# Q and K of two more row tiles as seven block products, and new places in the engines' lines

## The chip, the cores and the metric

The kernel runs on one core of one Trainium2 chip. Its time is the device time of one execution in microseconds (us), given as the median of several runs. Engines: PE (TensorE, matmuls), DVE (VectorE), ACT (ScalarE), POOL (GpSimd), SP (SyncE, which here only issues the transfers).

## The reference

One layer on x of 2048 rows by 512 columns, in float32: a layer norm, a local dilated attention, a second layer norm, and a GeGLU feed-forward part.

```python
qkv = layernorm(x) @ wqkv                       # 2048 x 1536: q, k, v; 32 heads of 16
idx = pos[:, None] - arange(8)[None, :] * 2     # each row sees 8 rows, 2 apart
attn = softmax(where(idx >= 0, (q . k[idx]) * 16 ** -0.5, -1e9))
h = x + (attn . v[idx]) @ wo
n = layernorm(h)
out = h + (gelu(n @ w_gate) * (n @ w_up)) @ w_down   # 512 -> 1792 -> 512
```

## The kernel before

**Tiles and chunks.** The 2048 rows are four chunks (c = 0 to 3) of 512, each of four row tiles (j = 0 to 3) of 128. The 512 columns are four blocks of 128 (k). The feed-forward part goes over 14 blocks of 128 of its 1792 columns.

**Matmuls in three parts.** Each float32 operand is held as a high part that the matmul unit takes as it is, and a low part, the rest: `split` (L343) makes both, the high one by a cast on ACT, the low one by a subtraction on DVE or POOL (L346). A product is then three matmuls, high by high, high by low and low by high. An output tile of 128 x 512 over 512 columns is 3 x 4 = 12 matmuls of 128x128 weights and 512 columns; the helper `mm` (L409, its matmuls at L424) issues them in three groups of four.

**The projections.** Rows are normalized and transposed to `xT` (high and low, `prep`, L517). V comes from `project` (L699), Q and K from `project_pair(c, p)` (L608), which takes the row tiles j0 = 2p and j1 = 2p + 1 together. For a pair, K and Q (s = 1 and 0) of two tiles are four outputs of 128 x 512. There are two branches. A pair in `PLAIN` takes the direct one: four outputs of twelve matmuls, each copied out by ACT (L625). Every other pair is seen as a 2 x 2 block product (tiles by halves of the columns, halves by Q and K) that is done in seven block products instead of eight, in Winograd's form: `product` (L642) is six matmuls (L649), three accumulators `qka`, `qkb`, `qkc` collect them, ACT copies four sums out (`scaled`, L661), and DVE adds three more onto what was copied (`added`, L666). The seven products need sums of the weights, made once (`weight_sums`, L567: wsa, wsb, then wT_2 to wT_5, split at L586 and L587), and for each pair sums of the rows (`sums`, L544): four additions of 128x256 (L554 to L557), two casts (L560) and two subtractions (L561) into `xS` and `xSl`. The sum wT_5 lies where weights of the direct branch lie (wh_0, wl_0), so as long as a pair is in `PLAIN` it is held back until that pair is through.

**The stages.** K and V go to memory, are read back at eight offsets (kw, vw), and `attention` (L725) works on DVE, POOL and ACT: `pk` = kw * qp (L762), a reduction to logits (L765), a softmax, `pv` = vw * probabilities (L806), halving additions (L811, L813). `tail(c)` (L835) turns the result to oT, multiplies by wo (high and low wo_h, wo_l), adds x, normalizes to `xhat_h` and transposes that (tp_h) to hT (hTh, hTl). In `ffn_step`, pg and pu are the gate and up products, g their combination, and acc the product with w_down. The attention of chunk 0 runs beside the projections of chunks 1 to 3; the later ones beside the feed-forward part of the chunk before. The feed-forward parts of chunks 2 and 3 run together for seven pairs of blocks (`joint`, L1026), again with seven products; `combine` (L995) makes the sums of rows for that (traw, L1011 to L1017, split to tt, tth and ttl at L1020 and L1021), tile after tile as the transposes of chunk 3 come.

**What sets the order.** The code doesn't emit instructions directly: each goes as an operation into `Plan`, with an engine, an estimated duration and what it reads and writes. `schedule` (L204) lists them by rank, the longest path to the end, engine by engine; on the chip each engine works its line in that order. Two tables adjust it: an entry of `SHIFTS` (first operation, how many, engines, nanoseconds) adds to the ranks of a run of operations, and a number in `SWAPS` puts an operation on its other engine (DVE or POOL for those added by `either`, ACT or DVE for those by `evict`). Transfers are all issued by SP.

Of the kernel before, what the change touches and what calls it, by code (L numbers as in the profile page):

```python
# [58 lines left out]
PLAIN = ((1, 0),)  # L59
# [9 lines left out]
    (1243, 51, "DVE POOL", 607), (1684, 47, "PE", 2887), (439, 11, "PE", -722), (1244, 116, "POOL", 519), (1484, 6, "DVE", 150411),  # L69
    (1712, 19, "PE", 3415), (1355, 6, "PE DVE ACT POOL SP", 453), (1818, 14, "DVE POOL", 1438), (420, 49, "DVE", -1515), (1271, 1, "DVE POOL", 1503),  # L70
    (805, 72, "PE DVE ACT POOL SP", 65), (1659, 45, "POOL", 4286), (1329, 5, "DVE POOL", 1248), (474, 21, "PE DVE ACT POOL SP", 83),
    (1945, 18, "PE", -716), (447, 33, "POOL", -774), (1674, 94, "PE DVE ACT POOL SP", 350), (438, 33, "DVE POOL", -523), (610, 3, "DVE", -1930),
    (1714, 11, "DVE POOL", -1835), (1574, 208, "DVE", -1090), (480, 8, "DVE", 431), (1306, 3, "DVE", -9919), (2055, 13, "PE DVE ACT POOL SP", 7868),
    (456, 2, "SP", 1705), (1285, 100, "POOL", -927), (476, 12, "POOL", -381), (452, 26, "PE", 4811), (809, 1, "PE DVE ACT POOL SP", 5603),
    (1354, 295, "SP", 347), (1358, 300, "POOL", 1339), (763, 183, "POOL", -78), (1185, 30, "DVE", 499), (1224, 84, "SP", -702),
    (890, 137, "POOL", 2449), (1739, 3, "ACT", 17332), (832, 16, "DVE", -177), (349, 16, "DVE", 8493), (198, 121, "SP", -12152),
    (1995, 136, "DVE", 10496), (1876, 12, "PE DVE ACT POOL SP", 603), (1865, 220, "DVE", 332), (1597, 2, "PE", 3205), (617, 37, "POOL", 446),
    (796, 2, "PE DVE ACT POOL SP", 4277), (693, 197, "PE", -649), (1304, 285, "DVE", -348), (1358, 129, "ACT", -838), (2054, 35, "DVE POOL", 9076),
    (1343, 13, "DVE", -308), (991, 177, "DVE", -621), (1335, 25, "POOL", 1698), (1202, 44, "PE", 121), (1172, 93, "DVE", -308), (1211, 3, "DVE", 830),
    (1052, 105, "ACT", -3324), (1261, 40, "DVE", -1436), (2058, 18, "PE", 8276), (2059, 1, "PE DVE ACT POOL SP", -15914),  # L80
    (113, 159, "PE DVE ACT POOL SP", 1041), (725, 67, "DVE POOL", -248), (826, 143, "SP", 1028), (573, 15, "PE DVE ACT POOL SP", 1449),
    (628, 3, "PE DVE ACT POOL SP", 1298), (1577, 7, "PE", -3666), (1370, 14, "PE", -1291), (305, 55, "ACT", 785), (832, 2, "PE DVE ACT POOL SP", 694),
    (266, 3, "DVE POOL", -4610), (986, 174, "DVE POOL", 371), (1209, 56, "SP", -365), (1093, 219, "SP", -672), (719, 170, "SP", -647),
    (1116, 2, "PE DVE ACT POOL SP", 506), (1227, 41, "DVE POOL", 71), (187, 75, "PE DVE ACT POOL SP", 2353), (1262, 42, "PE DVE ACT POOL SP", 530),
    (251, 3, "PE", -2556), (363, 3, "DVE POOL", -11034), (1802, 193, "DVE POOL", -111), (667, 6, "PE", -703), (1048, 234, "POOL", -100),
# [164 lines left out]
def tile_block(ctx: ExitStack, tc: tile.TileContext, x: bass.AP, xt: bass.AP, wqkv: bass.AP, wo: bass.AP,  # L250
# [266 lines left out]
    def prep(c, j):  # L517
        mb, mv = means[c]
        xc = raw(f"xc_{c}_{j}")
        if c in CROSS_X:  # L520
# [46 lines left out]
    def weight_sums():  # L567
# [9 lines left out]
        for i, (src, r, slot) in {3: (T1, (ra, 0), "gu0"), 4: (T2, (ra, 1), "more"), 2: (T4, (rb, 0), "wo_h"), 5: (T3, (rb, 1), None)}.items():  # L577
# [10 lines left out]

            if slot or not PLAIN:
                put()  # L590
# [17 lines left out]
    def project_pair(c, p):  # L608
# [5 lines left out]
        mv = means[c][1]  # L614
        if (c, p) in PLAIN:
            for s in (1, 0):
# [697 lines left out]
```

## Time and profile before

| | |
|---|---|
| median of 3 runs | 636.82 us (636.06 to 637.57) |
| the profiled execution, its own time | 637.77 us |
| its span | 636.0 us |
| TensorE clock granted, mean | 0.999 |
| first matmul of a projection, start | 11.62 us |
| last matmul, start | 631.59 us |

The span runs from the first to the last instruction that the profiler recorded; 1.77 us of the execution lie around it. "Busy" of an engine is the time in which it had an instruction at work. Matmuls overlap: a row of one matmul has 0.39 us, while the next starts 0.23 us after it, so PE's pace is read from starts. A row of the timeline is: start, duration, engine, line, operation, output<-inputs, shape, how many; in brackets the idle time of the engine just before it and what ended it. A row of the waits is: engine and line that waited, <- engine and line waited for, microseconds in total, times, the longest. Rows of grouped lines end in: busy time, mean ns of one, idle time before.

### The profile page before, as it was taken

Reading aid. Unit: us, or ns where it says so; the run is one execution under the profiler, and the core shown is the slowest. Engines: PE = TensorE matmul, PEld = TensorE weight load, DVE = VectorE, ACT = ScalarE, POOL = GpSimd, SP = SyncE. Lnnn points to the kernel's source line nnn. Section 1 sums busy time; section 2 is a strip of 40 time slices with the busy share of each in tenths; the row PEclk is TensorE's granted clock in tenths of the full one; section 3 lists DMA queues with packets and bytes.
Section 4 is the critical chain, followed back from the end, with each engine's and each line's share of the span. In section 5 each row is a group of like instructions: output and inputs, shape, how many; then the busy total and the mean of one; then the engine's idle time right before and its main releaser. Section 6 shows DMA issues by size and latency. Waiting matters only on the chain.

```text
span 636.0 us, 8302 instructions
## 1 busy us (share of the span) xinstructions
PE 627.6 (99%) x2794; PEld 514.8 (81%) x2794; DVE 490.2 (77%) x533; ACT 411.7 (65%) x702; POOL 390.0 (61%) x356
## 2 busy tenths in 40 slices
PE   9999999999999999999999999999999999999997
PEld 8888888877888887788888888887788888888885
DVE  5989999989999799989999999958775353343421
ACT  5796597457645954996876787976546555543542
POOL 4758788755799799344595882966737765720000
PEclk9999999999999999999999999999999999999999
DMA  8657697698879858999999689941232332212672
GB/s 307 235 196 267 207 259 216 193 361 279 321 245 290 280 190 230 291 330 371 336 294 330 184 260 251 262 133 36 88 107 103 116 99 84 66 51 54 197 223 89
DMA packets 74330, 134.04 MB, mean 211 GB/s; under 512 B 32288, under 2 KB 32544, under 8 KB 73904
## 3 DMA queue, kind: packets, MB, share of 16 engines
q1 hardware_dynamic: 74288, 133.51, 65.9%
q8 instruction: 22, 0.36, 0.2%
q14 instruction: 20, 0.16, 0.1%
HBM read 99.88 MB, written 26.80 MB: 199 GB/s over the span
## 4 chain that ended last, share of the span: by engine, by line
PE 79%; DVE 7%; DMA 4%; POOL 4%; ACT 4%; issue 1%; ACTq 0%; SPq 0%; DVEq 0%; POOLq 0%
PE pa L1086 10%; PE qkv L424 10%; PE pu L424 7%; PE pg L424 7%; PE acc L900 6%; PE acc L902 6%; PE acc L901 6%; PE pc L1086 5%; PE wo L424 5%; PE qka L649 4%; DMA fraw<-in_wffn_dram 2%; PE qkc L649 2%; PE qkv L417 2%; PE pb L1086 2%; PE warm_ps L332 2%
## 5 line engine op out<-in xcount | busy, mean ns | idle before, releaser
L811 POOL TENSOR_TENSOR pv<-pv 128x1024 f32<-128x1024 f32 (+1 forms) x46 | 92.2, 2012 | 21.3 <-DVE pv L806 20.6
L900 PE MATMUL acc<-dnh,gh 128*128 128x512 f32 x224 | 87.4, 390 | 0.0
L902 PE MATMUL acc<-dnh,gl 128*128 128x512 f32 x224 | 87.2, 389 | 0.0
L901 PE MATMUL acc<-dnl,gh 128*128 128x512 f32 x224 | 87.1, 389 | 0.0
L762 DVE TENSOR_TENSOR pk<-kw,qp 128x2048 f32<-128x2048 f32 x32 | 72.8, 2279 | 3.0 <-DMA kw<-kv 2.0
L806 DVE TENSOR_TENSOR pv<-vw,qp 128x2048 f32<-128x2048 f32 x32 | 72.7, 2281 | 0.9 <-ACT qp L785 0.5
L765 DVE TENSOR_REDUCE lg<-pk 128x128 f32<-128x2048 f32 x32 | 72.6, 2278 | 0.2
L424 PE MATMUL pg<-hTh,gu 128*128 128x512 f32 x224 | 60.2, 390 | 0.0
L424 PE MATMUL pu<-hTh,gu 128*128 128x512 f32 x224 | 59.9, 389 | 0.0
L424 PEld LDWEIGHTS pg<-hTh,gu 128*128 128x128 f32 x224 | 41.8, 188 | 9.6 <-ACT g L951 0.4
L900 PEld LDWEIGHTS acc<-dnh,gh 128*128 128x128 f32 x224 | 42.0, 188 | 9.0 <-ACT acc L304 0.2
L902 PEld LDWEIGHTS acc<-dnh,gl 128*128 128x128 f32 x224 | 42.1, 188 | 8.8
L424 PEld LDWEIGHTS pu<-hTh,gu 128*128 128x128 f32 x224 | 42.0, 188 | 8.8
L901 PEld LDWEIGHTS acc<-dnl,gh 128*128 128x128 f32 x224 | 42.1, 188 | 8.6
L346 POOL TENSOR_TENSOR gl<-g,gh 128x512 fp32r<-128x512 f32 x24 | 32.1, 1340 | 12.9 <-ACT gh L345 12.9
L1072 POOL TENSOR_TENSOR jl<-fraw,jh 128x256 fp32r<-128x256 f32 (+1 forms) x21 | 20.8, 994 | 27.6 <-ACT jh L1071 14.3
L345 ACT CAST gh<-g 128x512 fp32r<-128x512 f32 x42 | 26.0, 619 | 17.7 <-DVE g L957 9.8
L1118 ACT COPY jt<-pa 128x512 f32<-128x512 f32 x36 | 21.1, 587 | 24.8 <-PE pa L1086 20.2
L915 ACT CAST dnh<-fraw 128x512 fp32r<-128x512 f32 x42 | 25.9, 619 | 14.8 <-PE acc L902 8.8
L1086 PE MATMUL pa<-tt,jh 128*128 128x512 f32 x112 | 30.4, 393 | 1.4 <-ACT tt L1020 0.7
L1072 POOL TENSOR_TENSOR jl<-sraw,jh 128x512 fp32r<-128x512 f32 x21 | 27.3, 1302 | 6.6 <-ACT jh L1071 6.6
L346 POOL TENSOR_TENSOR gu<-fraw,gu 128x512 fp32r<-128x512 f32 x20 | 26.2, 1321 | 7.0 <-ACT gu L345 7.0
(312 smaller groups left out, 1600.2 us busy)
## 6 DMA issues: line engine op xcount, KB each, us to landing
fraw<-in_wffn_dram SPq DMA_DIRECT2D x45, 768.0 KB, 5.2
kw<-kv SPq DMA_DIRECT2D x16, 704.0 KB, 6.0
vw<-kv SPq DMA_DIRECT2D x16, 704.0 KB, 5.2
dnl<-ld SPq DMA_DIRECT2D x42, 256.0 KB, 3.0
gu<-ld SPq DMA_DIRECT2D x17, 512.0 KB, 5.4
kv<-qkvt SPq DMA_DIRECT2D x32, 256.0 KB, 4.2
ld<-gu SPq DMA_DIRECT2D x14, 512.0 KB, 4.5
x<-in_x_dram SPq DMA_DIRECT2D x16, 256.0 KB, 5.0
```

Source lines behind the costliest of these rows:

```text
L346: sub = lambda eng: eng.tensor_tensor(lo(), src(), hi().bitcast(F32), op=ALU.subtract)
L424: nc.tensor.matmul(acc(), a, b, start=(p == k == 0 and not seeded), stop=(p == n - 1 and k == KD - 1), skip_group_check=seeded)
L649: nc.tensor.matmul(acc(), a(k), b()[:, k], start=first and q == k == 0, stop=q == 2 and k == 1, skip_group_check=not first)
L762: nc.vector.tensor_tensor(pr(), k4, q2.unsqueeze(2).to_broadcast([P, 2, W, QF]), op=ALU.mult)
L765: dve(2195, lambda pr=pr, jj=jj: nc.vector.tensor_reduce(lg()[:, i, jj:jj + 2], pr().rearrange("p j w (h d) -> p j w h d", d=DH), axis=AX. ...
L806: nc.vector.tensor_tensor(pr().rearrange("p j w (h d) -> p j w h d", d=DH), v5, e5, op=ALU.mult)
L811: either(home, 256 * m, lambda eng, pr=pr, m=m: eng.tensor_tensor(pr()[:, :, 0:m], pr()[:, :, 0:m], pr()[:, :, m:2 * m], op=ALU.add), [], ...
L900: nc.tensor.matmul(a, gh()[:, sl], dh(), start=(i == 0 and not SEED), stop=False, skip_group_check=SEED)
L901: nc.tensor.matmul(a, gh()[:, sl], dl(), start=False, stop=False, skip_group_check=SEED)
L902: nc.tensor.matmul(a, gl()[:, sl], dh(), start=False, stop=(i == NF - 1), skip_group_check=SEED)
L1072: either("POOL", (hi - lo) * 256, lambda eng, src=src, v=v, W_=W_, L_=L_: eng.tensor_tensor(v(L_), src(), v(W_).bitcast(F32), op=ALU.subtr ...
L1086: nc.tensor.matmul(acc(), a[:, k], b(k), start=first and p == k == 0, stop=p == 2 and k == 1, skip_group_check=not first)
```

## The change

Line 59 empties `PLAIN`: the pair (1, 0), the first two row tiles of chunk 1, was the only one in the direct branch, and goes to the seven products like the other seven pairs. With it, `prep` calls `sums` for that pair too, and `weight_sums` splits wT_5 at once. The tables `SHIFTS` and `SWAPS` are renewed as a whole; the first has eight lines fewer, so that all lines behind it have numbers lower by 8.

```diff
-PLAIN = ((1, 0),)
+PLAIN = ()
...
-    (1243, 51, "DVE POOL", 607), (1684, 47, "PE", 2887), (439, 11, "PE", -722), (1244, 116, "POOL", 519), (1484, 6, "DVE", 150411),
...
+    (1249, 51, "DVE POOL", 607), (1250, 116, "POOL", 519), (1490, 6, "DVE", 150411), (1824, 14, "DVE POOL", 1410), (426, 49, "DVE", -670),
...
-    74, 81, 191, 194, 260, 262, 364, 365, 370, 372, 474, 484, 490, 491, 492, 494, 496, 571, 586, 602, 610, 613, 614, 615, 629, 640, 650, 652,
...
+    74, 77, 81, 92, 228, 262, 266, 267, 269, 370, 371, 376, 378, 387, 480, 490, 496, 497, 498, 500, 502, 577, 588, 592, 597, 606, 608, 619, 620,
...
```

PE's line has 2788 matmuls where it had 2794, DVE's 528 rows for 535, POOL's 376 for 361, ACT's 691 for 688; SP issues 328 transfers in both.

In the rows of the lines below, the chunk is left out of a name and a running number stands last.

The first place is PE's line between 45 and 60 us of the profile, where chunk 1 is projected. Before (qkv_1_0 is K of tile 0, qkv_0_1 Q of tile 1; qka_1 belongs to the second pair):

```order
L424 MATMUL qkv_0_1_613<-wh_242,xTh_1_536 128x512 x4
L424 MATMUL qkv_0_0_622<-wh_242,xTh_0_530 128x512 x4
L649 MATMUL qka_1_632<-wh_142,xTh_2_547 128x512 x2
L649 MATMUL qka_1_632<-wl_150,xTh_2_547 128x512 x2
L649 MATMUL qka_1_632<-wh_142,xTl_2_605 128x512 x2
L424 MATMUL qkv_0_0_622<-wl_254,xTh_0_530 128x512 x4
L424 MATMUL qkv_0_1_613<-wl_254,xTh_1_536 128x512 x4
L424 MATMUL qkv_0_0_622<-wh_242,xTl_0_586 128x512 x4
```

Of the change (qkc_0, qka_0 and qkb_0 belong to the first pair):

```order
L641 MATMUL qka_1_608<-wh_142,xTh_2_576 128x512 x2
L641 MATMUL qka_1_608<-wl_150,xTh_2_576 128x512 x2
L641 MATMUL qka_1_608<-wh_142,xTl_2_585 128x512 x2
L641 MATMUL qkc_0_621<-wT_304,xS_0_522 128x512 x4
L641 MATMUL qkc_0_621<-wT_304,xSl_0_539 128x512 x2
L416 MATMUL qkv_2_0_637<-wh_352,xTh_0_533 128x512 x4
L641 MATMUL qka_0_648<-wh_142,xTh_0_533 128x512 x2
L641 MATMUL qka_0_648<-wl_150,xTh_0_533 128x512 x2
L641 MATMUL qka_0_648<-wh_142,xTl_0_632 128x512 x2
```

The two pairs of chunk 1 now run mixed with one another, and twelve groups of four are replaced by seven products of six.

The second place is DVE's line ahead of wo of chunk 0, from 128 us on. Before (tp_o is the transposed attention output of the last tile, wor the wo weights as loaded):

```order
L666 SCALAR_TENSOR_TENSOR qkvt_1_1195<-qkb_1_1313,mvx_500,qkvt_1_1195 128x4x128
L762 TENSOR_TENSOR pk_1_0_1335<-kw_1_1080,qp 128x2048
L346 TENSOR_TENSOR oTl_1119<-tp_o_3_0_1338,oTh_1078 128x256
L666 SCALAR_TENSOR_TENSOR qkvt_0_1253<-qkc_1_1341,mvx_500,qkvt_0_1253 128x4x128
L346 TENSOR_TENSOR wo_l<-wor_998,wo_h 128x512
L346 TENSOR_TENSOR oTl_1119<-tp_o_3_2_1361,oTh_1078 128x256
L666 SCALAR_TENSOR_TENSOR qkvt_0_1253<-qkc_1_1341,mvx_500,qkvt_0_1253 128x4x128
L346 TENSOR_TENSOR wo_l<-wor_1013,wo_h 128x512
```

Of the change:

```order
L338 TENSOR_TENSOR oTl_1189<-tp_o_3_0_1307,oTh_1054 128x256
L805 TENSOR_TENSOR o_3_1295<-pv_3_2_1247 128x256
L658 SCALAR_TENSOR_TENSOR qkvt_1_1180<-qkb_1_1310,mvx_526,qkvt_1_1180 128x4x128
L754 TENSOR_TENSOR pk_1_0_1344<-kw_1_1065,qp 128x2048
L338 TENSOR_TENSOR oTl_1189<-tp_o_3_2_1334,oTh_1054 128x256
L658 SCALAR_TENSOR_TENSOR qkvt_0_1263<-qkc_0_1131,mvx_526,qkvt_0_1263 128x4x128
L658 SCALAR_TENSOR_TENSOR qkvt_0_1263<-qkc_1_1357,mvx_526,qkvt_0_1263 128x4x128
L338 TENSOR_TENSOR wo_l<-wor_991,wo_h 128x512
L338 TENSOR_TENSOR wo_l<-wor_1075,wo_h 128x512
```

The last oTl stands right behind pk, and the first wo_l split has gone behind it and behind two additions. o_3 (from POOL) is new on DVE ahead of pk.

The third place is DVE's line in the joint stage, from 440 us on, up to pa's multiplication by its mask (L1124; L1116 of the change). Before (traw_4187 belongs to tile 1, traw_4238 to tile 2, traw_4284 to tile 3):

```order
L405 TENSOR_SCALAR xhat_h_3_4254<-h_4049,mv_h_3_4227,rs_h_3_4232 128x512
L346 TENSOR_TENSOR hTl_4132<-tp_h_2_4222,hTh_4117 128x4x128
L1021 TENSOR_TENSOR tt_4148<-traw_4187,tt_4148 128x2x128
L1021 TENSOR_TENSOR tt_4152<-traw_4187,tt_4152 128x2x128
L1021 TENSOR_TENSOR ttl_4210<-traw_4187,tth_4197 128x2x128
L1011 TENSOR_TENSOR traw_4284<-tp_h_3_4270,hTh_3580 128x256
L1012 TENSOR_TENSOR traw_4284<-traw_4284,hTl_3605 128x256
```

Of the change (traw_4194, traw_4247 and traw_4295 are tiles 1 to 3):

```order
L338 TENSOR_TENSOR hTl_4135<-tp_h_2_4232,hTh_4124 128x4x128
L1006 TENSOR_TENSOR traw_4247<-tp_h_2_4232,traw_4247 128x256
L1007 TENSOR_TENSOR traw_4247<-tp_h_2_4232,traw_4247 128x256
L397 TENSOR_SCALAR xhat_h_3_4277<-h_4059,mv_h_3_4244,rs_h_3_4254 128x512
L1013 TENSOR_TENSOR tt_4150<-traw_4194,tt_4150 128x2x128
L1003 TENSOR_TENSOR traw_4295<-tp_h_3_4285,hTh_3571 128x256
L1004 TENSOR_TENSOR traw_4295<-traw_4295,hTl_3587 128x256
```

Two splits of tile 1 (tt_4152 and ttl_4210 of before) have gone to POOL. The splits and additions further on (tt and traw of tiles 2 and 3) are divided anew between DVE and POOL, too: two of them leave DVE ahead of L1124, and a 128x512 split (jl) comes in. On PE, the transpose tp_h of tile 3 stands three matmuls later.

More of the change, by code (lines that the diff above doesn't have):

```diff
@@ L73 @@
[L73 to L84, printed above, removed]
```

70 lines of the change are left out of this document (37 added, 33 removed), and 8 rows, old and new, of the table SWAPS.

## The prediction

> **What bounds the kernel now.** I read the page's first and fourth parts, then the windows by stage, the waits of TensorE (PE), and the timelines around the longest of them.
>
> ```profile
> span 636.0 us, 8302 instructions
> PE 627.6 (99%) x2794; PEld 514.8 (81%) x2794; DVE 490.2 (77%) x533; ACT 411.7 (65%) x702; POOL 390.0 (61%) x356
> ...
> PE 79%; DVE 7%; DMA 4%; POOL 4%; ACT 4%; issue 1%; ACTq 0%; SPq 0%; DVEq 0%; POOLq 0%
> ```
>
> PE is busy for 627.6 of 636.0 us, and the chain that ended last runs through PE for 79%. A matmul that disappears therefore shortens the span, unless PE then stands at a place where another engine is no earlier than before. The windows show where such places can be (the pairs are busy time and instructions of PE, PEld, DVE, ACT and POOL, then the clock, the DMA share and GB/s):
>
> ```profile
> 36.00:154.00 118.00, 117.43 (x524) 95.36 (x523) 112.39 (x111) 80.91 (x144) 84.05 (x75) 1.00 0.75 240
> 154.00:425.00 271.00, 270.25 (x1189) 221.91 (x1188) 250.42 (x231) 198.75 (x315) 193.05 (x154) 1.00 0.87 274
> 425.00:452.00 27.00, 25.33 (x114) 19.15 (x114) 23.59 (x51) 16.37 (x39) 17.59 (x25) 1.00 0.29 88
> 452.00:636.00 184.00, 179.93 (x792) 148.08 (x790) 77.68 (x109) 90.02 (x160) 72.90 (x76) 1.00 0.33 105
> ```
>
> The second stage (36 to 154 us: projections of chunks 1 to 3 beside the attention of chunk 0) has two full engines, PE with 0.57 us idle and DVE with 5.61 us idle. The 27 us from 425 on lose 1.67 us on PE, the densest loss of all; in the 271 us ahead of them PE lacks only 0.75 us. The clock is 1.00 in every stage, so nothing has to be allowed for it. The waits name the places:
>
> ```profile
> PE pa L1086 <- ACT tt L1020: 0.7, 1, 0.7
> PE pa L1086 <- ACT jt L1118: 0.7, 1, 0.7
> PE wo L424 <- DVE oTl L346: 0.4, 1, 0.4
> PE pg L424 <- DVE hTl L346: 0.2, 1, 0.2
> ```
>
> **Part 1: six matmuls fewer.** In the plain branch one output takes twelve matmuls:
>
> ```profile
> 57.23 1.07 PE L424 MATMUL qkv<-wh,xTh 128*128 128x512 f32 x4
> 58.14 1.07 PE L424 MATMUL qkv<-wl,xTh 128*128 128x512 f32 x4
> 59.05 1.07 PE L424 MATMUL qkv<-wh,xTl 128*128 128x512 f32 x4
> 59.95 0.62 PE L649 MATMUL qka<-wh,xS 128*128 128x512 f32 x2
> ```
>
> From 57.23 to 59.95 are 2.72 us for 12, or 0.2267 us each by start to start (the 0.39 us of a single row overlaps its neighbours). Four outputs are 48 matmuls; seven products of six are 42. All are 128x512 on 128*128 weights, as the last row shows for a product (L649). Six fewer are 6 x 0.2267 = **-1.36 us** of PE.
>
> **Part 2: what the products need.** Four 256-wide sums, two casts and two 512-wide subtractions for xS, three more additions (L666), and the fifth weight sum put at once, not after the pair. The four ACT copies of L625 become four of L661, in the same form. ACT has 37 us free in the stage (118.00 - 80.91), POOL 34 us; they hide two casts and whatever is on POOL. If that cover were gone, the casts alone would cost about 1.3 us. No DMA is added; SP has the same number. The stores of K and Q of chunk 1 stand behind the second pair as before, and its attention reads them past 120 us, so an addition that ends some us later holds no transfer.
>
> DVE is different, as it has no such room. I take three rows for the forms:
>
> ```profile
> L666 DVE SCALAR_TENSOR_TENSOR qkvt<-qkc,mvx,qkvt 128x512 f32<-128x512 f32 x10 | 7.4, 745 | 1.3 <-PE qkc L649 1.2
> ...
> L587 DVE TENSOR_TENSOR wT<-wsa,wT 128x1024 fp32r<-128x1024 f32 x1 | 1.2, 1218 | 0.0
> ...
> L557 DVE TENSOR_TENSOR xc<-xc 128x256 f32<-128x256 f32 x2 | 0.8, 414 | 0.0
> ```
>
> Between the first pk product and the last hTl of chunk 0, the new order puts on DVE three additions (2.24 us) and four 256-wide operations where two went away (+0.83 us); the 512-wide ones, two in and two out, cancel; one weight split goes ahead of the first pk (-1.22 us). The sum is +1.85 us of DVE work in a stage with 5.61 us of DVE idle. The larger savings (a 1024-wide difference and a 512-wide subtraction, now on POOL) lie ahead of the first pk, where DVE waits for a DMA anyway. I count them as nothing.
>
> **Part 3: the handover to wo.** PE stops in front of wo of chunk 0, which takes the bank that the transposed o is read from:
>
> ```profile
> 133.02 0.63 PE L649 MATMUL qkc<-wh,xS 128*128 128x512 f32 x2
> 134.04 2.13 PE L424 MATMUL wo<-wo_h,oTh 128*128 128x512 f32 x8 [0.39 <-DVE oTl L346]
> 136.01 1.07 PE L424 MATMUL wo<-wo_l,oTh 128*128 128x512 f32 x4
> ```
> ```profile
> 128.66 2.28 DVE L762 TENSOR_TENSOR pk<-kw,qp 128x2048 f32<-128x2048 f32 x1
> 130.85 0.42 DVE L346 TENSOR_TENSOR oTl<-tp_o,oTh 128x256 fp32r<-128x256 f32 x1
> 131.19 0.75 DVE L666 SCALAR_TENSOR_TENSOR qkvt<-qkc,mvx,qkvt 128x512 f32<-128x512 f32 x1
> 131.85 1.81 DVE L346 TENSOR_TENSOR wo_l<-wor,wo_h 128x512 fp32r<-128x512 f32 x1
> 133.58 0.41 DVE L346 TENSOR_TENSOR oTl<-tp_o,oTh 128x256 fp32r<-128x256 f32 x1
> ...
> 134.57 0.78 DVE L346 TENSOR_TENSOR wo_l<-wor,wo_h 128x512 fp32r<-128x512 f32 x1
> ```
>
> PE is through at 133.02 + 2 x 0.2267 = 133.47 and goes on at 134.04: 0.57 us lost, until the oTl of 133.58 has ended. In the new order this oTl stands right behind pk, ahead of the addition and the 1.81 us split. That wait goes. What is late next is wo_l: its two DVE splits now stand behind oTl and two additions. Six matmuls earlier, PE arrives at 132.11 and asks for the first wo_l at 132.11 + 8 x 0.2267 = 133.92. DVE, with oTl ending near 131.8, has 2 x 0.75 and a split of 0.78 to 1.81 in front of that: 134.1 to 135.1. The second split, 0.78 later (134.9 to 135.9), is asked for by the fourth matmul, at 134.6. So a new wait of 0.3 to 1.3 us stands against the 0.57 saved; I take 0.3, since 1.81 is a row with POOL beside it and 0.78 the usual one, hence 0.3 - 0.57 = **-0.27**, with about -0.5 and +0.7 as ends.
>
> The next place is pg of chunk 0, the first FFN matmul:
>
> ```profile
> 152.42 1.10 PE L424 MATMUL pg<-hTh,gu 128*128 128x512 f32 x4
> 153.70 1.20 PE L424 MATMUL pg<-hTl,gu 128*128 128x512 f32 x4 [0.18 <-DVE hTl L346]
> ```
>
> PE was ready at 152.42 + 4 x 0.2267 = 153.33, so 0.37 us are lost. The new order is as full of DVE work here as the old, so an hTl that isn't earlier by 1.36 us eats the gain of part 1. The ends: hTl as early as PE (-0.37), or 1.85 us later than before, when PE would lose 1.36 + 1.85. Part of the 5.61 us idle absorbs the load; by walking down the new order with old durations I find hTl near PE's new arrival, a little behind. I take **+0.5**.
>
> **Part 4: the joint stage.** Three stalls, one behind another:
>
> ```profile
> 440.76 0.39 PE L902 MATMUL acc<-dnh,gl 128*128 128x512 f32 x1
> 441.31 0.63 PE L357 MATMUL tp_h<-ident,xhat_h 128*128 128x128 f32 x4 [0.17 <-DVE hTl L346]
> ...
> 443.62 0.39 PE L902 MATMUL acc<-dnh,gl 128*128 128x512 f32 x1
> 444.71 1.36 PE L1086 MATMUL pa<-tt,jh 128*128 128x512 f32 x4 [0.71 <-ACT tt L1020]
> ...
> 447.39 0.62 PE L1086 MATMUL pc<-tt,jl 128*128 128x512 f32 x2
> 448.72 1.20 PE L1086 MATMUL pa<-tt,jh 128*128 128x512 f32 x4 [0.71 <-ACT jt L1118]
> ```
> ```profile
> 440.48 0.69 DVE L346 TENSOR_TENSOR hTl<-tp_h,hTh 128x512 fp32r<-128x512 f32 x1
> 441.08 1.29 DVE L1021 TENSOR_TENSOR tt<-traw,tt 128x256 fp32r<-128x256 f32 x2
> 442.30 0.41 DVE L1021 TENSOR_TENSOR ttl<-traw,tth 128x256 fp32r<-128x256 f32 x1
> 442.81 0.43 DVE L1011 TENSOR_TENSOR traw<-tp_h,hTh 128x256 f32<-128x256 f32 x1
> ```
>
> Against the pace PE loses 0.32 us at 441.31, 0.86 at 444.71 and 0.88 at 448.72, 2.06 together. The last transpose was done near 441.9, yet its combination on DVE began at 442.81, behind splits of tile 1 that nobody needed then. In the new order two of these three (one of the pair that took 1.29 us, which by the 0.41 of its like is some 0.9, and the 0.41) are on POOL, hTl stands ahead of two operations and the norm, and the transpose comes three matmuls later in PE's line. By the rows the combination then starts at PE's transpose, about 0.75 us earlier, which leaves 0.2 to 0.4 us of the second stall and none of the first. Of the third, two operations of 0.41 us ahead of DVE's L1124 go to POOL, one split of 0.68 us comes in; with the 0.75 inherited about 0.35 remains. That would be -1.3 to -1.5. POOL's queue is new in this chain, so I take **-1.1**; the ends are -2.06 (all gone) and +0.5 (POOL late).
>
> **Part 5: everything else.** Between 154 and 425 us only 0.75 us are there to win, and blocks of wo and their norms have been moved by 4 to some 50 matmuls. What I can't see there I put at **+0.3**, by the kind of stall that stands in such places now (0.2 to 0.9 us each), ends -0.7 and +1.5.
>
> **The sum:** -1.36 - 0.27 + 0.5 - 1.1 + 0.3 = -1.93 us. The profiled execution took 637.77 us, the span and 1.77 us around it; it becomes 635.84. The three runs shown have a median of 636.82, 0.95 below the profiled one, so the median becomes **634.9**.
>
> **Rivals.**
> Both handovers go well: DVE keeps PE's pace, and the stalls at wo and pg vanish. -1.36 - 0.57 - 0.37 - 1.3 + 0.3 = -3.3, or 633.5. DVE's 5.61 us of idle speaks for it, its +1.85 against. Chance 0.15.
>
> POOL gives nothing back. In part 4 and at wo, DVE operations stretch when POOL works beside them:
>
> ```profile
> 130.55 2.56 POOL L346 TENSOR_TENSOR wo_l<-wor,wo_h 128x512 fp32r<-128x512 f32 x2 [3.24 <-ACT wo_h L345]
> ```
>
> DVE's split of 131.85 took 1.81 us while POOL's second one ran (until 133.11), against 0.78 for the next. If every operation moved to POOL holds DVE up by as much as it saved, part 4 is worth 0: -1.36 - 0.27 + 0.5 + 0.3 = -0.8, or 636.0. The trace shows it for some pairs only. Chance 0.16. The Trainium skill states it as a rule (SBUF — State Buffer, Who interferes with whom): a VectorE instruction with two SBUF inputs contends with a GpSimd instruction that reads SBUF, and whoever comes first has the shared ports for its whole length. The 1.81 us agree with it. By that rule alone, the renewed places, which take operations off DVE for POOL, would bring no time, and the sum would be the one just given.
>
> PE's gain is eaten at pg, the joint stage goes as forecast: hTl ends about 1.0 us later than before, the gain of part 1 is lost, +1.0 + 0.3 - 1.1 = +0.2, or 637.0. Chance 0.13.
>
> Slower: DVE's added load of 1.85 us shows in full at hTl of chunk 0. It decides when the pg that needs hTl begins after 153.70 + 1.0 and POOL returns nothing, or after 155.8 with part 4 as forecast. Price: +1.85 + 0.3 - 0.6 = +1.55, or 638.4. The saturated row of the second stage speaks for it; the idle time that DVE spends there waiting for PE, which comes earlier, against. Chance 0.13.
>
> That the products aren't run, or cost as many matmuls, is excluded by the order: PE has 2788 rows of work for 2794.
>
> **How the numbers follow.** The forecast has 0.43, the rivals 0.15, 0.16, 0.13 and 0.13. A measurement of this kernel can tell about 0.2% (1.27 us, or 635.55 and 638.09) from no change. From the forecast's 0.43 I give 0.38 to faster, with all of the first rival and 0.02 of the second: 0.55. Same: 0.05 + 0.14 + 0.12 = 0.31. Slower: 0.13 and the 0.01 left: 0.14. The range takes in the first rival, with 0.3 us for the spread of the runs, and the three in the middle with theirs, and stops short of the slower one's price: 633.2 to 637.8.
>
> **What would show it.** PE x2788 and about 626.2 us busy (part 1). wo of chunk 0 starts near 132.1, with a wait on wo_l and none on oTl (part 3); the first pg with hTl starts near 152.5. tp_h of the last tile without a wait, the two pa waits at 0.5 us or less each (part 4). I am wrong in part 3 if the first pg is no earlier than 153.7; in part 4 if POOL ends the waits of pa; in part 5 if PE's idle time between 154 and 425 us exceeds 1.2 us.

## The result and the profile after

The changed kernel takes 639.83 us (median of 6 runs, 638.53 to 644.72) and the kernel before 637.01 (6 runs, 636.06 to 637.91): a ratio of 1.0054 with a 95% interval of 1.0031 to 1.0078. It is slower by about 2.8 us, where 634.9 was forecast. The profiled run took 640.54 us.

Numbers of lines below are those of the changed kernel, lower by 8 than in the prediction, unless a kernel is built on the one before. First the head of the page, the chain that ended last, and the windows of the changed kernel:

```profile
span 638.8 us, 8289 instructions
PE 625.7 (98%) x2788; PEld 514.6 (81%) x2788; DVE 486.5 (76%) x526; ACT 412.9 (65%) x705; POOL 402.9 (63%) x371
...
PE 85%; DVE 9%; ACT 2%; DMA 2%; issue 1%; SPq 0%; POOL 0%; ACTq 0%; DVEq 0%; POOLq 0%
```
```profile
36.00:154.00 118.00, 113.40 (x499) 92.00 (x498) 110.69 (x114) 79.02 (x140) 83.99 (x77) 0.99 0.73 232
154.00:425.00 271.00, 269.98 (x1190) 222.12 (x1189) 250.77 (x227) 199.76 (x317) 190.48 (x151) 1.00 0.89 277
425.00:452.00 27.00, 24.92 (x117) 19.52 (x115) 22.35 (x48) 17.26 (x40) 18.87 (x27) 1.00 0.26 88
```

The six matmuls are gone (x2788). But from 36 to 154 us PE now idles 118.00 - 113.40 = 4.60 us, where it was 0.57, and does 499 matmuls where it did 524. DVE is not fuller there than before (110.69 us, before 112.39), and neither is ACT (79.02, before 80.91). The waits of PE say for whom it stood:

```profile
PE qkv L416 <- ACT qkvt L707: 2.5, 1, 2.5
...
PE qka L641 <- ACT qkvt L653: 1.3, 1, 1.3
PE pa L1078 <- ACT tt L1012: 1.2, 1, 1.2
PE qkc L641 <- DVE qkvt L658: 0.8, 1, 0.8
```

Three of these are new and lie ahead of the feed-forward part: for ACT's copies of V and K out of the accumulators, and for one addition on DVE. None is at wo or pg, the two handovers that the prediction worked out. The timeline of PE around the longest:

```profile
99.13 1.19 PE L641 MATMUL qka<-wT,xTh 128*128 128x512 f32 x4 [1.26 <-ACT qkvt L653]
100.16 0.63 PE L641 MATMUL qka<-wT,xTl 128*128 128x512 f32 x2
...
105.61 0.61 PE L641 MATMUL qkc<-wT,xSl 128*128 128x512 f32 x2
108.73 2.07 PE L416 MATMUL qkv<-wh,xTh 128*128 128x512 f32 x4 [2.50 <-ACT qkvt L707]
110.60 1.72 PE L416 MATMUL qkv<-wl,xTh 128*128 128x512 f32 x4
112.16 1.09 PE L416 MATMUL qkv<-wh,xTl 128*128 128x512 f32 x4
```

The product at 100.16 is the last for K of chunk 2. It ends at 100.63, 24 more matmuls end at 106.07, and V of row tile 3 of chunk 2 starts at 108.73: 2.66 us lost. Its first eight matmuls then start 0.43 us apart (108.73 to 112.16), not 0.23: 1.6 us more. The chain that leads to 108.73, from the view of the chain within 84 to 112 us (start, duration, what):

```profile
83.56 2.20 DVE lg L757
85.75 0.34 DVE xc L546
...
86.16 0.75 POOL xc L547
...
86.94 0.02 ACT xS L552
...
89.88 1.00 ACT xc L361
90.88 0.04 ACT qp L747
90.92 6.25 DMA x<-xc
...
97.18 1.36 ACT xc L365
98.54 0.54 ACT qkvt L653
...
104.24 3.68 DMA kv<-qkvt
...
107.99 0.70 ACT qkvt L707
...
108.73 3.35 PE qkv L416 x7
```

Read upward. V's copy (107.99) writes the buffer that K of chunk 2 is stored from, so it waits for that store, which lands at 107.92. The store is late because K's copies (L653) stand in ACT's line behind copies of the transposed x of chunk 3 (L365), and the one at 97.18 waits for a transposing transfer of 6.25 us. That transfer is issued late, because the copy that feeds it (89.88) stands in ACT's line behind the cast of xS at 86.94, which waits for the sums of chunk 2, and the first of these (85.75) stands on DVE behind a reduction of 2.2 us (83.56). Before, this sum was POOL's and began eight us earlier:

```profile
77.78 0.74 POOL L554 TENSOR_TENSOR xc<-xc 128x256 f32<-128x256 f32 x1
```

So by this chain a sum of 0.4 us, put on another engine and eight us later, comes to PE at last, and no busy share shows it. It is read from one trace; no run below changes this sum alone. Before, the last K product ended at 94.51, and PE had 42 matmuls for the same chain of 8 us:

```profile
94.05 0.62 PE L649 MATMUL qka<-wT,xTl 128*128 128x512 f32 x2
94.51 0.61 PE L649 MATMUL qkb<-wh,xTh 128*128 128x512 f32 x2
...
103.74 0.62 PE L649 MATMUL qkc<-wh,xS 128*128 128x512 f32 x2
104.20 1.09 PE L424 MATMUL qkv<-wh,xTh 128*128 128x512 f32 x4
```

Last, wo and pg of chunk 0, and the joint stage:

```profile
136.39 0.74 PE L641 MATMUL qkc<-wh,xS 128*128 128x512 f32 x2 [0.84 <-DVE qkvt L658]
...
137.90 2.00 PE L416 MATMUL wo<-wo_h,oTh 128*128 128x512 f32 x8
...
156.27 1.10 PE L416 MATMUL pg<-hTh,gu 128*128 128x512 f32 x4
157.22 0.96 PE L416 MATMUL pg<-hTl,gu 128*128 128x512 f32 x3
...
445.53 0.60 PE L349 MATMUL tp_h<-ident,xhat_h 128*128 128x128 f32 x4
...
448.71 1.26 PE L1078 MATMUL pa<-tt,jh 128*128 128x512 f32 x4 [1.20 <-ACT tt L1012]
```

wo and pg begin without a wait, but wo at 137.90 (before 134.04) and pg at 156.27 (before 152.42). The loss of 3.85 us is made before either; behind pg the changed kernel wins back 1.1 us (last matmul 2.77 us later than before). In this run the first projection began at 11.06 us, before at 11.62. Counted from there, pg is 4.41 us late, and the sum nearly closes: 4.03 us more of idle time between 36 and 154 us, 1.6 us at half speed, less 1.36 us for the six matmuls, are 4.3 us.

### The profile page after: what moved, and what is told of

Same layout as the page of the kernel before. It is cut to its first block, busy times and chain, and to the rows that moved or that the text cites. A ratio compares the mean times of both kernels' runs of the same rounds, so it can differ in the third digit from the quotient of the medians.

```text
span 638.8 us, 8289 instructions
## 1 busy us (share of the span) xinstructions
PE 625.7 (98%) x2788; PEld 514.6 (81%) x2788; DVE 486.5 (76%) x526; ACT 412.9 (65%) x705; POOL 402.9 (63%) x371
## 2 busy tenths in 40 slices
DMA packets 74330, 134.04 MB, mean 210 GB/s; under 512 B 32288, under 2 KB 32544, under 8 KB 73904
## 4 chain that ended last, share of the span: by engine, by line
PE 85%; DVE 9%; ACT 2%; DMA 2%; issue 1%; SPq 0%; POOL 0%; ACTq 0%; DVEq 0%; POOLq 0%
PE pu L416 11%; PE pa L1078 10%; PE pg L416 10%; PE acc L892 7%; PE acc L894 7%; PE acc L893 7%; PE qkv L416 7%; PE wo L416 6%; PE pc L1078 6%; PE qka L641 3%; DVE pk L754 2%; DVE pv L798 2%; PE qkv L409 2%; PE pb L1078 2%; PE warm_ps L324 1%
```

## The experiments

The theory after this profile: the price lies in the places chosen for chunk 2 and 3, between 74 and 137 us. The rivals: the added work on DVE costs in any order; or the new places behind pg cost. Most kernels below run the operations in a list of my own instead of the planner's:

```diff
-        for o in plan.schedule():
-            o.emit()
+        for n in ORDER:
+            plan.ops[n].emit()
```

With it an order can be cut and joined: one kernel's list up to some point, then the other's. Each operation keeps the engine that the kernel has whose list it comes from.

All runs in one table. "Ratio" is to runs of the kernel before on the same chip. The last four columns are from the one profiled run: the start of a matmul less the start of the same one before (the first projection at 11.62 us, V of tile 3 of chunk 2 at 104.20, the first pg at 152.42, the last of all at 631.59). The column "first" says nothing of an edit: the matmuls ahead of the first projection (warm_ps) start 0.21 us apart to begin with and 0.11 us apart later, and this changes over at 7.16 us in the profiled run before and at 4.17 us in that of e3. To compare work, subtract it from the three columns behind it. Then e3, which up to pg is the kernel before, is level with it there (-0.11 us).

| run | us, median | ratio, 95% | first | V | pg | last |
|---|---|---|---|---|---|---|
| the change | 639.83 | 1.0054 (1.0031 to 1.0078) | -0.56 | +4.53 | +3.85 | +2.77 |
| e1_new_then_old | 639.30 | 1.0048 (1.0019 to 1.0077) | -0.54 | +3.35 | +3.32 | +4.60 |
| e2_new_until_pg | 641.34 | 1.0071 (1.0042 to 1.0101) | -0.82 | +4.51 | +2.32 | +2.12 |
| e3_old_until_pg | 636.98 | 1.0008 (0.9994 to 1.0021) | -1.44 | -1.53 | -1.55 | -2.27 |
| e4_new_old_new | 640.91 | 1.0059 (1.0042 to 1.0077) | -0.15 | +3.92 | +3.86 | +3.77 |
| e5_no_additions | 640.21 | 1.0055 (1.0035 to 1.0074) | -1.38 | +3.43 | +1.29 | +1.84 |
| e6_six_matmuls_less | 637.76 | 1.0016 (1.0002 to 1.0031) | -0.83 | -1.30 | -1.36 | +0.45 |
| e7_dve_load | 640.54 | 1.0057 (1.0036 to 1.0077) | -1.09 | +2.16 | +2.26 | +2.77 |
| e8_own_buffer | 639.15 | 1.0037 (1.0024 to 1.0050) | -0.46 | +1.75 | +2.03 | +3.34 |
| e9_early_prep | 652.46 | 1.0259 (1.0236 to 1.0282) | -0.74 | +13.02 | +14.18 | +14.15 |
| e10_prep_and_buffer | 650.57 | 1.0227 (1.0208 to 1.0245) | -1.25 | +11.89 | +13.04 | +12.13 |
| e11_split_earlier | 640.62 | 1.0071 (1.0051 to 1.0091) | -0.53 | +2.84 | +3.00 | +0.99 |
| e12_lines_rearranged | 646.80 | 1.0170 (1.0156 to 1.0184) | -0.50 | +1.02 | +6.67 | +9.07 |
| e13_before_rearranged | 646.58 | 1.0169 (1.0151 to 1.0186) | +0.02 | +3.50 | +10.13 | +9.98 |
| e14_relined_shared | 638.04 | 1.0027 (1.0013 to 1.0041) | -0.60 | +0.24 | +0.02 | -0.57 |
| e15_before_relined | 636.65 | 1.0006 (0.9993 to 1.0020) | -0.21 | -0.94 | -0.53 | +1.17 |
| e16_relined_no_additions | 637.49 | 1.0013 (0.9998 to 1.0027) | -0.46 | -0.20 | +0.27 | +0.09 |
| e17_before_relined_new_later | 637.13 | 1.0008 (0.9993 to 1.0022) | -0.27 | -1.02 | +0.87 | +0.34 |

### Which stretch of the lines: e1 to e4

Lists joined at 74 us or at the first pg: new then old, new up to pg then old, old (eight products) up to pg then new, and new, old, new.

> The changed program with the new lines up to about 74 us (chunk 1 with its seven products, and what they need) and the old lines from there on. Theory A (the loss is the new order of chunk 2 on PE and ACT between 74 and 156 us: K of its second pair is done some 6 us later, its stores hold up V's copies, and PE waits 1.4 and 2.7 us and then runs at half clock): the old lines don't have this, no wait of PE over 1 us is left in 74 to 156 us, and the six matmuls come through: 635.0 to 636.5. Theory B (the products themselves: three more additions and the sums make DVE late in the attention of chunk 0): 638 or more, with hTl or wo late behind DVE. Theory C (the new places from 156 us on): as A up to here.

> The changed program with the new lines up to the first pg of chunk 0 and the old ones from there on. A and B: as slow as the change or up to 1 us slower, 639.5 to 641, since in the change the part behind the first pg took 481.6 us against 482.3 before. C: 636 to 637.

> The program of before (twelve matmuls for each output of the pair) with the old lines up to the first pg of chunk 0 and the new ones from there on. A and B: 636.0 to 637.0, since the new places behind pg are worth about -0.7 us by the traces. C: 639 or more.

> As the first, but with the new lines again from the first pg of chunk 0 on. A: 0.7 us below the first, 634.3 to 635.8. B and C: 638 or more.

e3 has only the new places behind pg and can't be told from before. e2 has only the new lines ahead of it, with the products, and is as slow as the change. So the loss lies ahead of pg, and the renewed places behind it are worth nothing that can be measured. The old lines behind the new chunk 1 (e1) don't help either, and e4, which puts the new places behind pg to them, is no faster. In e1 PE waits in another place. DVE, then PE, of e1:

```profile
76.54 2.28 DVE L754 TENSOR_TENSOR pk<-kw,qp 128x2048 f32<-128x2048 f32 x1
...
79.19 4.47 DVE L757 TENSOR_REDUCE lg<-pk 128x128 f32<-128x2048 f32 x2
83.57 1.28 DVE L553 TENSOR_TENSOR xS<-xc,xS 128x512 fp32r<-128x512 f32 x1
```
```profile
84.91 1.22 PE L641 MATMUL qka<-wT,xS 128*128 128x512 f32 x2 [2.44 <-DVE xS L553]
```

The old line was made for a DVE that is 2.1 us earlier (there the split of xS starts at 81.48); behind two reductions of 2.2 us, a split of 1.28 us makes PE wait for 2.44. This bears out the rival in its time (638 or more), at another place than it named: DVE comes late out of the new chunk 1, and the old order has no room for that.

### The work by itself: e5, e6, e7

e5 is the change without the three additions of the new pair; e6 the kernel before with six matmuls less in the pair; e7 the kernel before with three DVE operations between 54 and 69 us issued twice, about 2.3 us more on DVE:

```diff
# e5, on the change
-            plan.ops[n].emit()
+            if n not in (310, 316, 320):
+                plan.ops[n].emit()
# e6, on before, in product()
-                for k, (a, b) in enumerate(triples[p]()):
+                for k, (a, b) in list(enumerate(triples[p]()))[SKIP.pop(0) if nm == "qk" and p == 1 and SKIP else 0:]:
...
+SKIP = [4, 2]
# e7, on before
-            o.emit()
+            for _ in range(2 if o.n in (314, 364, 572) else 1): o.emit()
```

> The changed program in its own order, with the three DVE additions of the pair (1, 0) left out (2.24 us of DVE between 54 and 70 us; K and Q of two tiles are then incomplete). Theory A (the waits at 99 and 109 us come from the order of ACT, the transposing transfers and K's stores): as the change, 639 to 641, both waits stand as they are. Theory B (DVE has no room for what the products add, and the two waits are that lateness, passed on): DVE is some 2 us earlier from 62 us on, the waits at 99 and 109 shrink by that or go, and the time falls to 635.5 to 637.5.

> The program of before, with six matmuls of the pair (1, 0) left out and nothing added (the high by low part of one output and half of another's; its K or Q is then less exact). If PE alone bounds the stage (part 1 of the prediction, and A): 637.0 - 1.4 = 635.3 to 636.0. If DVE bounds it as well (B): PE only stands earlier in front of xS, wo and pg, 636.4 to 637.2.

> The program of before, with three DVE operations between 54 and 69 us issued twice (a weight split, a reduction, a split of xT: 1.22 + 0.65 + 0.69 us less their overlap, some 2.3 us of DVE, the result unchanged). B: the lateness reaches PE at the sums of chunk 2 (xS, near 83 us), where before has no slack: 638.5 to 641, with a wait of PE of 1.5 to 2.5 us there. A: DVE's idle time takes it, 637.0 to 637.6.

e5, which leaves out 2.2 us of DVE work, is as slow as the change: with the new order, the additions aren't needed to lose. e7 is as slow too: with the old order, a load of 2.3 us on DVE is enough (PE waits 1.66 us for a split of a weight sum and 1.18 us for an addition, within 61 to 73 us, not near 83 as expected). Each alone suffices, so neither excludes the other. e6 is the gain by itself, and it is none. That PE reaches pg 1.36 us earlier is chance: its first projection began 0.83 us earlier, so only 0.53 us of the six matmuls are left at pg. PE first stands for an addition of DVE, and behind pg for a split that POOL does; before, it lost about 0.1 us at each of these two matmuls. PE of e6:

```profile
69.62 0.72 PE L649 MATMUL qkc<-wh,xS 128*128 128x512 f32 x2 [0.45 <-DVE qkvt L666]
...
198.00 1.20 PE L424 MATMUL pg<-hTh,gu 128*128 128x512 f32 x4 [0.92 <-POOL gu L346]
```

### Taking out single waits: e8 to e11

e8 gives V of chunk 2 a buffer that doesn't hold K (that of wo_l, not yet in use). e9 puts the preparation of chunk 2 (tiles 2 and 3) and chunk 3 back to its old places and the sum of L546 to POOL; e10 is both. e11 is e1 with DVE's split of xS ahead of the reductions.

```diff
-            qkvt[c, s] = ring("qkvt", 2, [P, NQ, J, QF], name=f"qkvt_{c}_{s}", at=lambda k: f"v{k}")
+            qkvt[c, s] = T("wo_l", [P, NQ, J, QF], name=f"qkvt_{c}_{s}") if c == 2 and ... else ring(...)
```

> The changed program in its own order, with V of chunk 2 in a buffer of its own (the place that wo_l takes later), so that its copies don't wait for K's stores. A: the wait of 2.66 us in front of V at 108.7 us goes, and the half clock behind it, 636 to 637.5. B: the wait goes too, but part of it comes back where DVE is late (qkc of chunk 3, wo, pg): 637.5 to 639.

> The change, with one thing put back: the preparation of the x tiles 2 and 3 of chunk 2 and of chunk 3 (their casts, splits, sums, rotations and transposes on ACT, DVE, POOL and SP) stands at the places, and the first sum of xc_2_3 on the engine, that it had before the change; TensorE's line, and all else, stays the change's. Theory A (the new places let the preparation come up to 6 us late: xS_2_1 cast at 86.94 instead of 80.50 us, xS_3_0 at 109.15 instead of 103.97): the wait of 1.42 us at qka_2_1 goes, and those of 1.0 us at chunk 3 too; the wait of 2.66 us at V of tile 3 of chunk 2 stays, since 24 matmuls (5.44 us) stand between K's last product and it, and the chain of copy, store and copy takes 8.1 us; first wo product about 2.4 us earlier than in the change (135.5 us), time 637.4. Rival B (the three added additions load DVE, whatever the places): what is earlier here makes something else late, the first wo product stays near 137.9 and the time at 639 or above.

> As e9_early_prep, and V of chunk 2 has a buffer of its own (wo_l's, not yet in use), so that its copies don't wait for K's stores. Theory A: the 2.66 us at V of tile 3 and the eight matmuls at half speed behind it (1.56 us) go too, and the wait doesn't come back at xS_3_0 as it did with the buffer alone, since chunk 3's preparation is early: first wo product at 131.5 to 133.5 us, time 635.0 to 636.5, below that of before. Rival B: the wait comes back elsewhere ahead of the first wo product; time 638.5 or above.

> As e1_new_then_old (the change's lines to 74 us, the lines of before behind), with a few instructions around 75 us put earlier: DVE does the split of xS_2_0 ahead of the two reduces of lg instead of behind them, ACT casts xS_2_0 and xTh_2_2 first, TensorE ends V of tile 2 of chunk 1 ahead of tile 3. Theory A (a fixed load of about 2 us on DVE costs only where DVE's line has the split that TensorE waits for behind long attention work): the 2.60 us at qka_2_0 and the 1.55 us at half speed behind it go, and most of the 1.42 at xTh_2_2; first wo product within 133 to 134.3 us instead of 137.4; the time 635.5 to 637, since e1's waits at pg_0_6 and wo_1_3 (about 2 us) may stay. Rival B (the load costs at the next thing that DVE owes, wherever that is): the wait comes back within 30 us, first wo product near 137, time 639.

All four missed: where the wait that was aimed at went, another came. In e8 the 2.66 us went, and PE waits 0.84, 1.05 and 0.78 us at 98.80, 112.69 and 121.09, each for a copy of K by ACT. In e11 it waits 2.00 us at 86.98, again for ACT. In e10 not even the wait at V of tile 3 went, though V has its own buffer there:

```profile
116.09 1.21 PE L416 MATMUL qkv<-wh,xTh 128*128 128x512 f32 x4 [1.90 <-ACT qkvt L707]
```

In e9 the earlier preparation made it far worse. ACT, then PE, of e9:

```profile
91.06 1.04 ACT L361 COPY xc<-x 128x1024 uint16<-128x1024 uint16 x1 [0.83 <-POOL xS L553]
92.01 0.68 ACT L653 ACTIVATE qkvt<-qka,mvx 128x512 f32<-128x512 f32 x1
```
```profile
92.75 1.22 PE L641 MATMUL qka<-wh,xS 128*128 128x512 f32 x2 [6.63 <-ACT qkvt L653]
```

A copy for chunk 3 (91.06) now stood in ACT's line ahead of K's copy and had to wait for POOL, and PE waited 6.63 us behind both. These four settle no cause: none of these waits could be taken out by itself, and the chain read from the changed kernel's trace is not confirmed by them.

### The whole stretch in another order: e12 to e17

Here the orders between 62 and 152 us are chosen by moving operations in a reckoning of the five lines, in which an operation starts when its engine is free and its inputs are there. e12 and e14 do so for the change, e13 and e15 for the kernel before; operations, engines and buffers stay.

> The change, all its operations on the same engines and with the same buffers, but the order of each engine's line between 62 and 152 us chosen anew, so that TensorE never waits for a copy there by the durations and landing times that the profiles show (K's copies and the preparation of chunk 2 and 3 ahead of attention work, other products between K's last product and V of tile 3). Outside that stretch each line is the change's. Theory A (what the change lost lies in the order of the lines from 74 to 137 us, not in the three additions or the weight sums as such): the waits of 1.42, 2.66 and 1.01 us and the 1.56 us at half speed go; first pg product at 149.7 to 151.5 us instead of 156.27, 2 us ahead of before's 152.42; from there on 481.5 to 483 us as in both; time 634 to 636.5, 635 the likeliest. Rival B (the added work on DVE costs in any order): first pg not before 154.5 and the time 638.5 or above. Rival C (PE's earliness is lost again behind pg, where POOL's and DVE's work for the gate products sets the pace, as with the six matmuls less): first pg early, but 636 to 637.5.

> The control to e12_lines_rearranged: the kernel before with its own lines between 62 and 152 us chosen anew in the same manner. It has six matmuls more and three additions less than e12. Theory A: before had no long wait there (0.57 us of TensorE idle from 36 to 154 us), so there is nearly nothing to win: 636 to 637, and e12 is below it by 0.5 to 1.5 us (six matmuls are 1.36 us). If the search itself, not the change's fewer matmuls, is what makes e12 fast, then this one is as fast as e12 or faster.

Both came out 10 us above before. The reckoning had left out that DVE and POOL can hold each other up. POOL and DVE of e12:

```profile
64.23 2.41 POOL L803 TENSOR_TENSOR pv<-pv 128x1024 f32<-128x1024 f32 x1 [1.57 <-DVE pv L798]
```
```profile
64.65 2.54 DVE L338 TENSOR_TENSOR xTl<-xc,xTh 128x512 fp32r<-128x512 f32 x1
67.23 1.40 DVE L546 TENSOR_TENSOR xc<-xc 128x256 f32<-128x256 f32 x1
```

The split takes 2.54 us beside POOL's addition; in the changed kernel the same one takes 0.68 us (at 69.73). This agrees with the rule of the Trainium skill (SBUF — State Buffer, Who interferes with whom) that the prediction named: two inputs in SBUF on VectorE and a reading GpSimd exclude each other. With such operations made to exclude each other, the same reckoning gives the change's own waits and most of e12's loss (5.7 us at pg, measured 6.67), and the orders were chosen again:

> As e12_lines_rearranged (the change's operations, engines and buffers, another order from 62 to 152 us), but this order was chosen with what e12 and e13 showed and their choice had left out: while DVE adds or subtracts float32 tiles held in SBUF, POOL's like operations stand still, and the other way round, so their times add up. Reckoned that way the change's own order gives its waits (1.24, 2.97 and 0.99 us; measured 1.42, 2.66, 1.01) and e12's loss (5.7 us at the first pg product; measured 6.7), and the new order brings the first pg product 4.3 to 5.1 us ahead of the change's. Theory A (the order alone made the loss): first pg product at 149.5 to 152 us instead of 156.27, also without the 1.56 us at half speed; time 633.5 to 636.5. Rival B (the added work on DVE and POOL costs in any order): first pg at 153.5 or later, time 638 or above.

> The control to e14_relined_shared: the kernel before, its order from 62 to 152 us chosen anew in the same manner. By the same reckoning its first pg product comes 1.7 to 3.6 us earlier than in before (152.42), thus at 149 to 151 us and no later than e14's although it has six matmuls more: 633.5 to 636. Theory A': if it is as fast as e14 or faster, the six matmuls saved are worth nothing here, because DVE and POOL, whose operations add up, set the pace together with TensorE, and the three additions take from them what the matmuls give. Rival: e14 is below it by 1 us or more, so the six matmuls do reach the end once the order lets them.

The windows of e14, then PE at pg:

```profile
36.00:154.00 118.00, 116.08 (x517) 93.57 (x516) 112.51 (x118) 81.19 (x145) 85.48 (x78) 1.00 0.69 231
```
```profile
145.53 0.66 PE L349 MATMUL tp_h<-ident,xhat_h 128*128 128x128 f32 x4 [0.54 <-DVE hTl L338]
...
152.44 1.10 PE L416 MATMUL pg<-hTh,gu 128*128 128x512 f32 x4
```

With the same operations on the same engines, pg starts at 152.44 instead of 156.27: by these two profiles, whose first projections start within 0.04 us of each other, the order is worth 3.8 us there. The waits of 1.3 and 2.5 us and the half speed are gone (PE idle 1.92 us in the stage, not 4.60). The times show less. The median of e14 is 1.8 us below the change's, in the range that the rival gave (638 or above), though pg is earlier than the rival had it, and its interval still lies above 1. And the three runs of the change with a mean clock of 0.999, thus without the half speed, have a median of 638.72 us, 1.7 us above before; e14 is 1.6 us above the runs of before on its chip. So by the times the new order saves the half speed, and no more than that is shown. e15, the kernel before in a new order, stays where before is and 1.4 us below e14, though it has six matmuls more. Two more runs asked for the rest:

> e14_relined_shared without the three additions that DVE does for the row tiles 0 and 1 of chunk 1 (a part of K and Q of those two tiles is left out), everything else in e14's order. e14 has its first pg product where before has it (152.44 us), although it has six matmuls less (1.36 us). Theory A (the additions, 1.9 us on DVE, are what takes the six matmuls' gain back there): first pg product 1 to 2 us earlier than e14's, near 151, and 636.0 to 637.2. Rival B (what is left in e14 is order as well, waits at V of chunk 1 and at chunk 3 that have nothing to do with the additions): within 0.5 us of e14 at the first pg product, 637.5 to 638.5.

> The kernel before (eight products, no additions) with e15_before_relined's order up to the first pg product and the change's order from there on. e15 reached the first pg product 0.53 us ahead of before and lost 2.2 us at pu_0_9, wo_1_0 and wo_1_3 behind it (0.94, 0.55, 0.83 us); the change's order lost nothing from pg to the end against before (481.6 against 482.3 us), nor did e3. Theory: both add up, 635 to 636, below before and the change by 0.5 us or more. Rival: waits of 1 us behind pg come in any order, since DVE and POOL are busy there 9 parts of 10, and this is as before: 636.2 to 637.2.

Without the additions e14 is no faster at pg (152.69); PE comes earlier to the transpose of the second norm and waits 1.26 us there for DVE's hTl instead of 0.54. The ratios of the two (1.0013 and 1.0027) have intervals that overlap, so what the additions cost in this order, if anything, isn't settled. e17 gained nothing. No version found here beats the kernel before.

## Why the prediction was wrong

**Part 1, six matmuls: the count was right, the step from there to the time was not.** PE does 2788. In e6, counted from the first projection, 0.53 of the 1.36 us arrive at pg; the rest is lost on the way (DVE's addition at 69.62), and what arrives is lost again (POOL's split at 198.00, then ACT's copy ahead of wo, 1.00 us at 259.80). The end comes 1.27 us later than before. The prediction argued from 99% busy that "a matmul that disappears therefore shortens the span", unless PE then stands where another engine is no earlier, and then looked for such places at three points only. e6 meets three more of them, each with another engine: the other engines' lines are just in time in many places.

**Parts 2 and 3, "Six matmuls earlier, PE arrives at 132.11": this is the step that failed.** The way from the pair to wo, where the tables had put the work on chunks 2 and 3 in a new order, has no term in the sum; it counts as nothing lost. What the prediction has in favour of that is part 2's comparison of busy shares (ACT with 37 us free, POOL with 34, "they hide two casts and whatever is on POOL"). PE came to wo at 137.90: it idled 4.60 us between 36 and 154 us where it had idled 0.57, and did eight matmuls at half speed (1.6 us). ACT is as free in the changed kernel, and PE still waits 3.8 us for two of its copies, since a copy in ACT's line can't pass one that waits for a transfer or for POOL. The sum of +1.85 us on DVE was no better a measure: DVE is not fuller afterwards, and the chain to the longest wait goes back to one sum that is eight us later in its line. That a like load costs in the old order is shown by e7; that the change is as slow without its additions, by e5.

**Part 3, the handovers themselves.** Both waits went, and the one on wo_l that I added never came: -0.57 and -0.37, better than the -0.27 and +0.5 I took. But PE came nearly six us later than I let it, so the two places were not put to the test at the time that I gave. I never walked PE's line between 60 and 133 us, where it fell behind (V of tile 3 of chunk 2 by 4.53 us). The prediction's own test (first pg no earlier than 153.7) says wrong in part 3: it came at 156.27.

**Part 4, the joint stage: -1.1 forecast, about nothing found.** The transpose of the last tile has no wait, the third wait fell from 0.7 to 0.2 as reckoned, but the second grew from 0.7 to 1.2: from the transpose to pa are 3.18 us (445.53 to 448.71), before 3.40, and PE has three matmuls less to fill them, because the transpose was put behind these. The profile names ACT, but POOL has its part. DVE began the combination right at the transpose, as reckoned; its second addition then took 1.01 us, with one of POOL's beside it, where before it took 0.42:

```profile
446.68 1.01 DVE L1004 TENSOR_TENSOR traw<-traw,hTl 128x256 f32<-128x256 f32 x1
```
```profile
446.67 0.74 POOL L1009 TENSOR_TENSOR traw<-traw,hTl 128x256 f32<-128x256 f32 x1
```

**Part 5** was right in size: PE idles 1.02 us between 154 and 425, 0.27 more than before, against +0.3. Parts 4 and 5 together, -0.8 in the sum, are -0.7 from pg to the last matmul in e3's profile and -1.1 in the change's, of which 0.5 came behind the joint stage's stalls, where none was forecast; e3's median shows none of it.

**The rivals.** The slower one (638.4) had the sign and nearly the size for a wrong reason: its mechanism, hTl late at pg, isn't there. POOL giving nothing back (636.0) is not what decided the time, but its mechanism is there: by the rows above, 0.6 us of the second stall of part 4, and more in e12.

**What is shown, and what stays open.** Shown: the loss lies ahead of pg (e2, e3); the three additions aren't needed for it (e5); the half speed behind the 2.5 us wait is part of it, and another order of the same work avoids that (e14). Read from traces, but confirmed by no run: the chain from the late sum to that wait. Not settled: the 1.6 us by which e14's median is above before's. Its profiled run hides them, as it is 0.83 us below e14's median and that of before 0.76 us above its own. It is not settled either whether the added work on DVE costs something in any order, or whether some order lets the 1.36 us through. The new orders reach from 62 to 152 us and only move operations within their lines; a choice of engines anew was not tried.

## What to carry to other kernels

A busy share of 65% on an engine says nothing of the next copy that TensorE needs: walk TensorE's line through the whole stretch that is reordered, and for each accumulator that it takes next ask what stands in the copying engine's line ahead of that copy, and what that waits for. Where one engine is full to 99% and the others' lines are just in time, a little work taken off it can be worth nothing by itself, as in e6. Compare traces from a common event, not from the start of the span: 0.83 of e6's 1.36 us were there before the first projection. And when a table of places is renewed with an edit, run the edit with the old places and the places without the edit: here two runs (e2, e3) told more than the sum.

## What was not expected of the hardware

**A wait of 2.5 us can cost half as much again.** The granted clock of the changed kernel around the long wait, in windows of 3.4 us or less:

```profile
105.00:108.00 3.00, 1.23 (x6) 0.69 (x4) 2.58 (x3) 1.95 (x3) 2.54 (x2) 1.00 1.04 398
108.60:112.00 3.40, 3.27 (x8) 2.59 (x9) 2.88 (x4) 1.66 (x5) 3.40 (x4) 0.51 0.38 109
112.00:115.40 3.40, 3.40 (x17) 2.76 (x16) 2.38 (x5) 2.07 (x4) 0.47 (x1) 1.00 0.80 276
```

Eight matmuls at 0.51 of the clock, 0.43 us from start to start, then full speed. The same stood behind waits of 2.44 us in e1, 6.63 in e9, 2.35 in e13 and 1.90 in e10 (0.51 from 117.3 to 120.8 us), but not behind 2.65 us in e2 and 2.41 in e5. The Trainium skill (TensorE: Matmul & The Clock Gate, Part 1) has a gate that halves the clock after an idle window of about 3.4 us, with windows that run freely. The 0.51 agrees with the half, and the 0.43 us with the 426.7 ns that it gives for this width; but idle times of 1.90 to 2.5 us, well under one window, were enough here in some runs and not in others. The changed kernel's runs with a mean clock of 0.999 took 638.53 to 639.14 us, those with 0.996 and 0.997 took 640.51 to 644.72: part of its spread is this.

**How much the order alone is worth.** Same operations, engines and buffers: 638.0 us (e14), 639.8 (the change), 646.8 (e12). The whole arithmetic in question is 1.36 us.
